# One core: w_out's sums beside w_in2's, joint low parts on GpSimd, w_out's loads a quarter step later

## The chip, the cores and the metric

The program runs on one core of a Trainium2 chip. Its time is the device time of one execution in microseconds (us). A core has TensorE (PE), which multiplies, VectorE (DVE), ScalarE (ACT) and GpSimd (POOL), which work on tiles, and queues that start DMA transfers: nearly all of them are started by SyncE (SP), a few by ACT. The program gives each engine and each queue a list of its own, and the trace shows its instructions in that order.

## The reference

```python
scores = (q @ k.T) / sqrt(64); ret = scores * gamma ** (i - j) for i >= j, else 0   # 8 x 8 heads, 576 positions
x = (ret @ v) as 4608 x 512
h = x @ w_in (512 x 2048);  g = h * sigmoid(1.702 * h);  x2 = g @ w_out (2048 x 512)
h = x2 @ w_in2;             g = h - tanh(h);             out = g @ w_out2
```

All data is float32. A product is taken as three passes on TensorE: each operand is split into a high part (fp32r, by a copy on ACT) and a low part (the operand less its high part, a subtraction), and high by high, high by low and low by high are summed.

## The kernel before

**Blocks and steps.** The 4608 tokens are 9 blocks of 512, and the 2048 columns of w_in are 16 chunks of 128. The first MLP's input products (`mm_in`, line 616, 12 matmuls each) are 144 steps, numbered by n; the main loop runs n = 32 to 143, and a step can be counted in the trace by its group of 12 L616 matmuls. Beside them the loop carries the rest of the attention (`attn_visit`, steps with even n up to 124), the decoding of the packed weights (`dec_piece`, a few pieces per step), the activation `act_a` (tanh on ACT, line 630, and a product on VectorE, line 632) and, for n = 34 to 81, the output products of the first three blocks (`out_units`, line 812, four units of three matmuls per step).

**Weights that are made on the way.** Some blocks are multiplied by a scheme with seven products in place of eight (Strassen's form), which needs sums and differences of parts of the weights. Two generators make them and are advanced once per step by `some(prep, 1)`: `w2_prep` forms those of w_in2 (its subtractions on GpSimd, line 960; copies and low parts at lines 938 and 939) and stores them as `wq`; `t_prep` forms those of w_out (half-tile subtractions on VectorE, line 995; copies and low parts at lines 990 and 991) and stores them as `wt`. They are chained: `t_prep` starts when `w2_prep` has ended. By the program's order `w2_prep` works in steps 49 to 104 and `t_prep` in steps 105 to 131. Each has 8 rounds. Both use the four halves of `room` in turn, and so does `sums`.

**The summed blocks.** In steps 96 to 111 and 128 to 143 (`SUMMED`), `sums` forms five operands of 128x512 from the activations of two blocks for every two steps (lines 1233 to 1236) and `stores` sends them to DRAM (line 1206, `gs`); the activations of other late blocks go there too (line 659, `gd`). A tile `t` that act_a writes is free for the next but two only when its store has landed.

**After the main loop** the second MLP's input products (lines 1046 and 1059) and the output products (`out_units`) take turns, a few units at a time. A step of `out_units` is four units of three matmuls. The steps that follow the first three blocks are: two more single blocks (line 812), then the joint stage of 56 steps for four blocks at once (`mm_joint`, line 753; seven stages of eight steps), then single blocks again (line 816). In the joint stage every step needs two activations: each is loaded (`g_load`, line 723, into one of five buffers), copied on ACT (line 728) and subtracted on VectorE (line 729) by `act_b`. At the end of a stage `evac_joint` empties the four accumulators; in the last five stages VectorE does it (line 786), adding a `kept` tile that `kept_load` (line 770) fetched when five steps of the stage were done. Before an accumulator is emptied, the next stage's first matmuls into it can't start, where that stage begins afresh.

**Order of the loads.** `w_ahead(k)` starts the load of the weights of a later step (line 272; line 286 in the joint stage: two steps ahead, into the slot that the step before the present one has read). It stands at the start of step k, ahead of `g_ahead`, which starts the loads of activations and their splits. All of these are SP's, so a load that waits for its slot holds up whatever stands behind it.

```python
def w_ahead(k):                   # out_units calls it first in a step
    if joint(k + 2): wj_load(k + 2 - N1)
    while n_w[0] <= min(k + 3, n_steps - 1): ... wo_load(n_w[0])
def g_ahead(x):
    while ... n_g[0] <= ...: g_load(n_g[0])      # SP: load
    while ... n_b[0] < n_items: act_b(n_b[0])    # ACT copy, then the low part
```

## Time and profile before

| | |
|---|---|
| three runs | 1701.92, 1705.47, 1706.06 us; median 1705.47 |
| profiled execution | 1705.2 us, its span 1703.4 us |
| TensorE busy | 1651.0 us (97%), mean granted clock 0.99 |
| VectorE, ScalarE, GpSimd busy | 1228.3 us (72%), 886.6 us (52%), 110.6 us (6%) |
| DMA | 510.60 MB, mean 300 GB/s |

The span runs from the first to the last instruction; 1.8 us of the time lie outside it. A busy time is the sum of an engine's instructions; the time of the whole follows the engine that waits least, here TensorE, and so the waits of TensorE and the stretches in which it does fewer matmuls than elsewhere are what there is to read. Lines are those of the kernel before.

### The profile page before, as it was taken

What the parts mean: (1) busy time and instruction counts of PE and PEld (TensorE: products, weight loads), DVE (VectorE), ACT (ScalarE), POOL (GpSimd) and SP (SyncE); (2) the same over time, 40 slices, a digit from 0 to 9 for tenths busy, and PEclk for the clock granted to TensorE, in tenths of its full rate; (3) what the DMA queues carried; (4) which work ended last, traced back from release to release, by engine and by line L of the source; (5) the groups of instructions that cost most, each with busy time, mean ns of one, the idle gap of its engine ahead of it and who ended that gap; (6) DMA issues with size and microseconds to landing.
All of it is one profiled execution on the core that took longest, in us unless ns stands there. A gap on an engine that the chain in (4) does not pass through costs nothing.

```text
span 1703.4 us, 25300 instructions
## 1 busy us (share of the span) xinstructions
PE 1651.0 (97%) x8874; PEld 1342.8 (79%) x8874; DVE 1228.3 (72%) x1958; ACT 886.6 (52%) x1633; POOL 110.6 (6%) x99
## 2 busy tenths in 40 slices
PE   7999999999999998899999998999999999999999
PEld 4787888887888787688778777778888888888887
DVE  6787887778877866567678887777876777766632
ACT  5443433434433232456677666656665676656632
POOL 2101001212123100000000000000000000000000
PEclk9999999999999999999999999999999999999999
DMA  9666679888899989998899988989899988989962
GB/s 274 180 211 228 226 262 326 285 293 324 310 351 337 363 316 362 325 340 281 296 347 313 342 292 312 342 286 359 307 328 346 316 303 312 320 304 311 360 212 87
DMA packets 195503, 510.60 MB, mean 300 GB/s; under 512 B 21808, under 2 KB 31152, under 8 KB 186416
## 3 DMA queue, kind: packets, MB, share of 16 engines
q1 hardware_dynamic: 182704, 486.88, 82.2%
q10 hardware_dynamic: 12672, 22.11, 3.5%
q8 instruction: 70, 1.15, 0.3%
q14 instruction: 57, 0.47, 0.1%
HBM read 361.05 MB, written 147.85 MB: 299 GB/s over the span
## 4 chain that ended last, share of the span: by engine, by line
PE 75%; DMA 12%; DVE 8%; ACT 2%; issue 2%; SPq 1%; ACTq 0%; DVEq 0%
PE acc L816 23%; PE h L616 14%; PE acc L812 12%; PE x L1059 8%; PE acc L753 5%; PE y L1059 4%; PE h L1046 2%; PE w L1059 2%; DMA gs<-spare 2%; DMA gs<-t 1%; DMA gl<-gs 1%; DMA wos<-wd 1%; PE pat L538 1%; DMA gl<-gd 1%; DVE t L632 1%
## 5 line engine op out<-in xcount | busy, mean ns | idle before, releaser
L616 PE MATMUL h<-xh,wi 128*128 128x512 f32 x1152 | 372.3, 394 | 6.6 <-DVE t L632 5.8
L816 PE MATMUL acc<-wos,g 128*128 128x512 f32 x1344 | 329.6, 390 | 4.0 <-DVE kept L786 3.9
L816 PEld LDWEIGHTS acc<-wos,g 128*128 128x128 f32 x1344 | 252.4, 188 | 57.4 <-DVE kept L786 4.4
L728 ACT ACTIVATE g<-gl 128x512 fp32r<-128x512 f32 x222 | 139.3, 628 | 268.1 <-PE acc L816 173.2
L616 PEld LDWEIGHTS h<-xh,wi 128*128 128x128 f32 x1152 | 217.3, 189 | 56.3 <-DVE t L632 7.1
L729 DVE TENSOR_TENSOR g<-gl,g 128x512 fp32r<-128x512 f32 x222 | 152.1, 686 | 147.0 <-ACT g L728 146.4
L616 PE MATMUL h<-xl,wi 128*128 128x512 f32 x576 | 225.4, 391 | 0.4 <-DVE xl L445 0.4
L1059 PE MATMUL x<-xo,wq 128*128 128x512 f32 x768 | 195.1, 389 | 1.3 <-DVE h L1339 1.3
L812 PE MATMUL acc<-g,wos 128*128 128x512 f32 x768 | 189.0, 396 | 6.2 <-DMA wos<-wd 5.9
L812 PEld LDWEIGHTS acc<-g,wos 128*128 128x128 f32 x768 | 144.4, 190 | 39.2 <-issue 7.5
L1059 PEld LDWEIGHTS x<-xo,wq 128*128 128x128 f32 x768 | 144.0, 188 | 32.0 <-DVE h L1339 2.1
L131 ACT ACTIVATE e<-e,ebias 128x512 int32<-128x512 int32 x64 | 46.4, 724 | 208.1 <-DVE e L129 202.8
L632 DVE SCALAR_TENSOR_TENSOR t<-t,h 128x512 f32<-128x512 f32 x144 | 97.6, 682 | 54.4 <-ACT t L630 54.2
L653 DVE SCALAR_TENSOR_TENSOR pl<-pl,sq 128x512 f32<-128x512 f32 x144 | 99.5, 691 | 39.6 <-ACT pl L650 37.4
L630 ACT ACTIVATE t<-h 128x512 f32<-128x512 f32 x144 | 83.4, 587 | 85.1 <-PE h L616 59.9
L616 PEld LDWEIGHTS h<-xl,wi 128*128 128x128 f32 x576 | 108.7, 189 | 22.9 <-DVE xl L445 1.1
L655 DVE COPY_PREDICATED t<-marks,pl 128x512 f32<-128x512 int32 x144 | 109.4, 760 | 14.8
L753 PE MATMUL acc<-g,wos 128*128 128x512 f32 x408 | 104.9, 396 | 12.5 <-issue 3.7
L650 ACT ACTIVATE pl<-sq,abias 128x512 f32<-128x512 f32 x144 | 104.3, 724 | 4.7
L651 ACT ACTIVATE marks<-sq,sbias 128x512 f32<-128x512 f32 x144 | 102.0, 708 | 0.0
L753 PEld LDWEIGHTS acc<-g,wos 128*128 128x128 f32 x408 | 77.2, 191 | 31.2 <-issue 13.0
L1059 PE MATMUL y<-xo,wq 128*128 128x512 f32 x384 | 99.3, 395 | 0.0
(129 smaller groups left out, 2301.1 us busy)
## 6 DMA issues: line engine op xcount, KB each, us to landing
wos<-wd SPq DMA_DIRECT2D x176, 512.0 KB, 5.6
gd<-t SPq DMA_DIRECT2D x208, 256.0 KB, 5.2
gl<-gd SPq DMA_DIRECT2D x202, 256.0 KB, 5.3
wq<-wq SPq DMA_DIRECT2D x32, 1024.0 KB, 7.4
at<-in_attn_dram SPq DMA_DIRECT2D x29, 1024.0 KB, 6.6
stg<-in_w_dram SPq DMA_DIRECT2D x48, 512.0 KB, 6.7
wq<-wq SPq DMA_DIRECT2D x32, 768.0 KB, 8.9
wd<-ws SPq DMA_DIRECT2D x32, 512.0 KB, 5.4
```

Of the source, the lines that this page charges most:

```text
L616: nc.tensor.matmul(h, lhsT=win[f][:, a, k], rhs=xs[b][:, k], start=(n == 0), stop=(n == 3 * KD - 1))
L632: nc.vector.scalar_tensor_tensor(out=t, in0=t, scalar=1.0, in1=h, op0=ALU.add, op1=ALU.mult)
L650: nc.scalar.activation(out=pl, in_=sq, func=ACTF.Square, bias=abias)
L651: nc.scalar.activation(out=small, in_=sq, func=ACTF.Relu, bias=sbias, scale=-1.0)
L653: nc.vector.scalar_tensor_tensor(out=pl, in0=pl, scalar=CB, in1=sq, op0=ALU.add, op1=ALU.mult)
L655: nc.vector.copy_predicated(out=t, mask=small.bitcast(I32), data=pl)
L728: nc.scalar.activation(out=g[:, 0], in_=t, func=ACTF.Copy)
L729: nc.vector.tensor_tensor(out=g[:, 1], in0=t, in1=g[:, 0].bitcast(F32), op=ALU.subtract)
L753: nc.tensor.matmul(acc[y], lhsT=wo[:, a, m * P:(m + 1) * P], rhs=g[:, b], start=fresh and q == 0 and n == 0, stop=q == NF // 2 - 1 and n = ...
L812: nc.tensor.matmul(acc[m], lhsT=wh[:, m // 2, a, m % 2 * P:(m % 2 + 1) * P], rhs=g[:, b], start=first, stop=last)
L816: nc.tensor.matmul(acc[m], lhsT=g[:, a, c], rhs=wo[:, b], start=first, stop=last)
L1059: nc.tensor.matmul(ps, lhsT=wq[q][t][:, o // 2, o % 2 * 2 + k, a], rhs=xo[i][k][:, b], start=first and n == 0, stop=n == 5, skip_group_che ...
```

## The change

Four things are changed. `t_prep` is no longer chained behind `w2_prep`: both are advanced in every step, and `t_prep` starts a round when the decoding has come far enough, as `w2_prep` does. By the program's order it now works in steps 49 to 88, and `w2_prep`, with one more `yield` in a round, in steps 49 to 112. Buffers move with that: `w2_prep` loads into the fourth half of `room`, both share the other three, `t_prep` loads into the tiles `gl`, and `sums` writes into tiles `stg`. The low parts of the joint stage's activations are formed on GpSimd. In a step of `out_units`, `w_ahead` stands after the first unit (ahead of `mm_out(o, 1)` or `mm_joint(k, 1)`), behind `g_ahead`; `kept_load` stands ahead of the step's fourth unit.

```diff
@@ -726,7 +726,8 @@
         t = tt.pop(step_of(x)) if x < DIRECT * NF else gl.pop(x)
         gt[x] = g = g_place(x)
         nc.scalar.activation(out=g[:, 0], in_=t, func=ACTF.Copy)
-        nc.vector.tensor_tensor(out=g[:, 1], in0=t, in1=g[:, 0].bitcast(F32), op=ALU.subtract)
+        eng = nc.gpsimd if joint_item(x) else nc.vector
+        eng.tensor_tensor(out=g[:, 1], in0=t, in1=g[:, 0].bitcast(F32), op=ALU.subtract)
 
     STAGES = (
         ("a11", ("o", 0, 0), True, None, "m1"),
@@ -880,12 +881,14 @@
     def out_units():
 
         for k in range(n_steps):
-            w_ahead(k)
             if joint(k):
-                kept_load(k)
                 for y in range(4):
                     if y % 2 == 0:
                         g_ahead(N1 + 2 * (k - N1) + y // 2)
+                    if y == 1:
+                        w_ahead(k)
+                    if y == 3:
+                        kept_load(k)
                     mm_joint(k, y)
                     if (k - N1) % (NF // 2) == NF // 2 - 1:
                         evac_joint(k, y)
@@ -894,6 +897,8 @@
             g_ahead(k if k < N1 else k + NJ)
             o = plain(k)
             for m in range(4):
+                if m == 1:
+                    w_ahead(k)
                 mm_out(o, m)
                 if o % NF == NF - 1:
                     evac(o, m)
@@ -931,7 +936,7 @@
                 )
 
         def halves_of(n, src):
-            sv = room[seen["room"] % 4]
+            sv = room[seen["room"] % 3]
             seen["room"] += 1
             kv = sv.rearrange("p a (k c) -> p (a k) c", c=2 * P).rearrange("p k (a c) -> p k a c", a=2)
             src = src.rearrange("p (k c) -> p k c", k=KD)
@@ -940,7 +945,8 @@
             waiting.append((n, sv))
 
         def load(q):
-            raw[q] = [t_p.tile([P, DM], F32, tag="gl", name="wr", bufs=2) for _ in range(2)]
+            t = room[3].bitcast(F32)
+            raw[q] = [t[:, 0], t[:, 1]]
             for i in range(2):
                 nc.sync.dma_start(out=raw[q][i], in_=w2_d[q + i * NF // 2])
 
@@ -948,6 +954,7 @@
             while n_dec[0] < 3 * (2 * NF + 2 * q + 3):
                 yield
             load(q)
+            yield
             yield
             wq_d[q] = dram.tile([P, 8 * DM], F32, tag=f"wq{q}", name="wq")
             lo, hi = raw.pop(q)
@@ -983,7 +990,7 @@
                 )
 
         def halves_of(n, src):
-            sv = room[seen["room"] % 4]
+            sv = room[seen["room"] % 3]
             seen["room"] += 1
             kv = by_half(sv)
             src = columns(src)
@@ -993,18 +1000,17 @@
 
         h = slice(0, DM // 2), slice(DM // 2, DM)
         sub = lambda o, a, b: nc.vector.tensor_tensor(out=o, in0=a, in1=b, op=ALU.subtract)
-        def load(q):
-            t = raw[q] = st_p.tile([P, 2, DM], F32, tag="stg", name="wr", bufs=3)
+        while not room:
+            yield
+        for q in range(NF // 2):
+            while n_dec[0] < 3 * (NF + q + NF // 2 + 3):
+                yield
+            wt_d[q] = dram.tile([P, 4 * DM], F32, tag=f"wt{q}", name="wt")
+            lo, hi = ts = [t_p.tile([P, DM], F32, tag="gl", name="wr", bufs=2) for _ in range(2)]
             for i in range(2):
-                nc.sync.dma_start(out=t[:, i], in_=r_d[q + i * NF // 2])
-
-        for q in range(2):
-            load(q)
-            yield
-        for q in range(NF // 2):
-            wt_d[q] = dram.tile([P, 4 * DM], F32, tag=f"wt{q}", name="wt")
-            t = raw.pop(q)
-            lo, hi = t[:, 0], t[:, 1]
+                nc.sync.dma_start(out=ts[i], in_=r_d[q + i * NF // 2])
+            yield
+            yield
             sub(lo[:, h[0]], lo[:, h[1]], lo[:, h[0]])
             sub(lo[:, h[1]], hi[:, h[1]], lo[:, h[1]])
             yield
@@ -1014,8 +1020,6 @@
             yield
             store()
             halves_of(1, hi)
-            if q + 2 < NF // 2:
-                load(q + 2)
             yield
             store()
 
@@ -1227,8 +1231,7 @@
         j = SUMMED[b]
         a11, a12 = firsts.pop(u)
         a21, a22 = (tt.pop(j * NF + q + i * NF // 2) for i in range(2))
-        s = room[seen["room"] % 4].bitcast(F32)
-        seen["room"] += 1
+        s = st_p.tile([P, 2, BLK], F32, tag="stg", name="s12", bufs=3)
         s1, s2 = s[:, 0], s[:, 1]
         nc.vector.tensor_tensor(out=s1, in0=a21, in1=a22, op=ALU.add)
         nc.vector.tensor_tensor(out=s2, in0=s1, in1=a11, op=ALU.subtract)
@@ -1242,7 +1245,7 @@
 
     room = []
     seen["room"] = 0
-    prep = chain(w2_prep(), t_prep())
+    prep, prep_t = w2_prep(), t_prep()
     std = x2_std()
     xo_tag += [f"wi{f}" for f in range(NF)] + ["ws", "ws"]
     outs = out_units()
@@ -1288,6 +1291,7 @@
             spare = [x_p.tile([P, 2, 2, DM], F32R, tag="y", name="spare", bufs=2) for _ in range(2)]
             room += [spare[i][:, k] for k in range(2) for i in range(2)]
         some(prep, 1)
+        some(prep_t, 1)
         if n == NB * NF - 6:
             w_ahead(DIRECT * NF - 2)
             while n_g[0] < DIRECT * NF + 3:
```

`w2_prep`'s `halves_of`, too, takes `seen["room"] % 3`. TensorE's order is the same in both programs. Three places show what moves elsewhere.

VectorE, end of step 50, and step 51, of the main loop (`L632` begins what a step adds; `L939` and `L944` are w_in2's low parts, `L1002` and `L998` w_out's subtractions and low parts). Before:

```order
L729 TENSOR_TENSOR g<-t,g 128x512
L137 SCALAR_TENSOR_TENSOR z<-stg,z 128x512
L939 TENSOR_TENSOR spare<-wr,spare 128x4x128
L143 SCALAR_TENSOR_TENSOR e<-stg,e 128x512
L148 TENSOR_TENSOR z<-z,e 128x512
L632 SCALAR_TENSOR_TENSOR t<-t,h 128x512
L729 TENSOR_TENSOR g<-t,g 128x512
L129 TENSOR_SCALAR e<-stg 128x512
L132 TENSOR_SCALAR z<-stg 128x512
L137 SCALAR_TENSOR_TENSOR z<-stg,z 128x512
L939 TENSOR_TENSOR spare<-wr,spare 128x4x128
L556 TENSOR_TENSOR xl<-pat,xh 128x4x128
```

and now:

```order
L1002 TENSOR_TENSOR wr<-wr 128x256 x2
L143 SCALAR_TENSOR_TENSOR e<-stg,e 128x512
L148 TENSOR_TENSOR z<-z,e 128x512
L632 SCALAR_TENSOR_TENSOR t<-t,h 128x512
L730 TENSOR_TENSOR g<-t,g 128x512
L129 TENSOR_SCALAR e<-stg 128x512
L132 TENSOR_SCALAR z<-stg 128x512
L137 SCALAR_TENSOR_TENSOR z<-stg,z 128x512
L944 TENSOR_TENSOR spare<-spare 128x4x128
L1002 TENSOR_TENSOR wr<-wr 128x256 x2
L998 TENSOR_TENSOR spare<-wr,spare 128x2x256
L556 TENSOR_TENSOR xl<-pat,xh 128x4x128
```

Two pairs of half-tile subtractions and a low part of w_out now stand here, behind step 50's and step 51's activation.

VectorE at the first stage end with kept tiles (`L786` and `L787` empty the accumulators; `L729` is a low part of the joint stage; the rest is the activation of the second MLP). Before:

```order
L729 TENSOR_TENSOR wos<-gl,wos 128x512 x2
L1339 TENSOR_TENSOR h_9029<-y,u_8990 128x512
L729 TENSOR_TENSOR g<-gl,g 128x512
L1339 TENSOR_TENSOR h_9052<-x,m_8955 128x512
L729 TENSOR_TENSOR g<-wos,g 128x512
L729 TENSOR_TENSOR g<-gl,g 128x512
L786 SCALAR_TENSOR_TENSOR kept<-acc_8759,kept 128x512
L649 TENSOR_TENSOR t<-h_9029,t 128x512
L653 SCALAR_TENSOR_TENSOR pl<-pl,sq 128x512
L654 SCALAR_TENSOR_TENSOR pl<-pl,h_9029 128x512
L655 COPY_PREDICATED t<-marks,pl 128x512
L1339 TENSOR_TENSOR h_9097<-w,m_8914 128x512
```

and now:

```order
L1343 TENSOR_TENSOR h_9029<-y,u_8998 128x512
L1343 TENSOR_TENSOR h_9060<-x,m_8962 128x512
L787 SCALAR_TENSOR_TENSOR kept<-acc_8766,kept 128x512
L649 TENSOR_TENSOR t<-h_9029,t 128x512
L653 SCALAR_TENSOR_TENSOR pl<-pl,sq 128x512
L654 SCALAR_TENSOR_TENSOR pl<-pl,h_9029 128x512
L655 COPY_PREDICATED t<-marks,pl 128x512
L1343 TENSOR_TENSOR h_9104<-w,m_8922 128x512
```

The low parts (`L729`) are gone from VectorE's order; nothing has come in their place.

SP at the same stage end (`gl` and `wos<-gs` are loads of activations, `wos<-wt` those of weights, `gd` the stores of activations, `wq` the weights of w_in2). Before:

```order
L659 DMA gd<-t 128x512
L723 DMA gl<-gs 128x512
L659 DMA gd<-t 128x512
L286 DMA wos<-wt 128x512
L770 DMA kept<-kept 128x512 x2
L770 DMA t<-kept 128x512 x2
L723 DMA wos<-gs 128x512
L723 DMA gl<-gs 128x512
L1036 DMA wq<-wq 128x2048
L1036 DMA wq<-wq 128x1536
L286 DMA wos<-wt 128x512
L723 DMA gl<-gs 128x512 x2
```

and now:

```order
L659 DMA gd<-t 128x512
L723 DMA wos<-gs 128x512
L286 DMA wos<-wt 128x512
L723 DMA gl<-gs 128x512
L1040 DMA wq<-wq 128x2048
L1040 DMA wq<-wq 128x1536
L771 DMA kept<-kept 128x512 x2
L771 DMA t<-kept 128x512 x2
L723 DMA gl<-gs 128x512
L286 DMA wos<-wt 128x512
L723 DMA gl<-gs 128x512 x2
```

The kept tiles' four loads have moved behind a load of weights, two of activations and the two big loads of `wq`.

## Rows read from the trace of the kernel before

**Rows 1.** Page: the span, and mean GB/s in forty equal slices.
```profile
span 1703.4 us, 25300 instructions
...
GB/s 274 180 211 228 226 262 326 285 293 324 310 351 337 363 316 362 325 340 281 296 347 313 342 292 312 342 286 359 307 328 346 316 303 312 320 304 311 360 212 87
```

**Rows 2.** Busy time by stretch, with matmul counts, clock and DMA; columns in line one.
```profile
core 0: us, PE busy (x) PEld busy (x) DVE busy (x) ACT busy (x) POOL busy (x), PEclk, DMA share, GB/s
272.00:500.00 228.00, 227.70 (x1461) 184.08 (x1460) 185.95 (x302) 95.63 (x182) 47.68 (x43) 1.00 0.87 312
500.00:590.00 90.00, 88.45 (x687) 71.97 (x686) 65.05 (x106) 27.23 (x61) 22.41 (x20) 1.00 0.99 353
660.00:720.00 60.00, 48.97 (x192) 39.15 (x191) 32.08 (x50) 18.30 (x32) 0.00 (x0) 0.89 0.95 341
720.00:820.00 100.00, 100.00 (x443) 82.81 (x442) 65.28 (x96) 55.19 (x95) 0.00 (x0) 1.00 0.87 315
820.00:1120.00 300.00, 279.47 (x1197) 226.10 (x1196) 234.57 (x360) 200.21 (x349) 0.00 (x0) 0.98 0.91 318
1120.00:1600.00 480.00, 480.00 (x2120) 397.44 (x2119) 350.00 (x523) 311.72 (x539) 0.00 (x0) 1.00 0.92 322
```

**Rows 3.** Waits of TensorE, 500 to 1120 us: total, times, longest.
```profile
PE acc L812 <- DMA wos<-wd: 5.9, 1, 5.9
PE h L616 <- DVE t L632: 5.8, 2, 4.2
PE acc L753 <- DVE t L786: 4.8, 4, 2.9
PE acc L816 <- DVE kept L786: 3.9, 1, 3.9
PE acc L753 <- issue: 3.7, 1, 3.7
```

**Rows 4.** Timeline, 660 to 700 us: start, duration, instruction, idle time before it.
```profile
671.32 1.08 ACT L630 ACTIVATE t<-h 128x512 f32<-128x512 f32 x2 [7.06 <-DMA gs<-t]
...
689.02 1.26 SPq L272 DMA_DIRECT2D wos<-wd  x2
...
698.57 5.46 PE L812 MATMUL acc<-g,wos 128*128 128x512 f32 x12 [5.92 <-DMA wos<-wd]
```

**Rows 5.** Timeline at 387 us: a split on VectorE and the matmuls after it.
```profile
386.51 0.68 DVE L729 TENSOR_TENSOR g<-t,g 128x512 fp32r<-128x512 f32 x1
...
387.42 1.75 PE L812 MATMUL acc<-g,wos 128*128 128x512 f32 x7
```

**Rows 6.** VectorE by line and form, 500 to 660 us: count, busy, mean ns.
```profile
L995 DVE TENSOR_TENSOR wr<-wr 128x256 f32<-128x256 f32 x32 | 13.5, 421 | 0.6
L991 DVE TENSOR_TENSOR spare<-wr,spare 128x512 fp32r<-128x512 f32 x16 | 11.0, 686 | 5.3 <-ACT spare L990 5.3
```

**Rows 7.** The same, 820 to 1120 us.
```profile
L729 DVE TENSOR_TENSOR g<-gl,g 128x512 fp32r<-128x512 f32 x52 | 35.7, 686 | 12.4 <-ACT g L728 12.2
...
L655 DVE COPY_PREDICATED t<-marks,pl 128x512 f32<-128x512 int32 x43 | 32.6, 759 | 4.4
```

**Rows 8.** GpSimd by line and form, whole span.
```profile
L332 POOL TENSOR_TENSOR at<-at,qt_sb 128x512 f32<-128x512 f32 x33 | 46.3, 1404 | 317.6 <-DMA at<-in_attn_dram 302.7 <-PE h L616 8.6 <-PE pe L428 6.3
```

**Rows 9.** Timeline: the same VectorE instruction beside GpSimd and without it.
```profile
559.20 1.30 POOL L332 TENSOR_TENSOR at<-at,qt_sb 128x512 f32<-128x512 f32 x1 [11.65 <-DMA at<-in_attn_dram]
...
559.21 1.83 DVE L1234 TENSOR_TENSOR spare<-spare,a 128x512 f32<-128x512 f32 x1
...
643.92 0.69 DVE L1234 TENSOR_TENSOR spare<-spare,a 128x512 f32<-128x512 f32 x1
```

**Rows 10.** Timeline at the first stage end with kept tiles.
```profile
935.54 0.98 SPq L770 DMA_DIRECT2D kept<-kept  x2
...
938.71 1.71 SPq L1036 DMA_DIRECT2D wq<-wq  x2
...
945.82 0.69 DVE L786 SCALAR_TENSOR_TENSOR kept<-acc,kept 128x512 f32<-128x512 f32 x1
```

More of the change, by code (lines that the diff above doesn't have):

```diff
@@ L1 @@
 from contextlib import ExitStack
-from itertools import chain, islice
+from itertools import islice
 import concourse.bass as bass
@@ L995, in t_prep @@
         sub = lambda o, a, b: nc.vector.tensor_tensor(out=o, in0=a, in1=b, op=ALU.subtract)
-        def load(q):
-            t = raw[q] = st_p.tile([P, 2, DM], F32, tag="stg", name="wr", bufs=3)
-            for i in range(2):
-                nc.sync.dma_start(out=t[:, i], in_=r_d[q + i * NF // 2])
-        for q in range(2):
-            load(q)
+        while not room:
             yield
         for q in range(NF // 2):
+            while n_dec[0] < 3 * (NF + q + NF // 2 + 3):
+                yield
             wt_d[q] = dram.tile([P, 4 * DM], F32, tag=f"wt{q}", name="wt")
-            t = raw.pop(q)
-            lo, hi = t[:, 0], t[:, 1]
+            lo, hi = ts = [t_p.tile([P, DM], F32, tag="gl", name="wr", bufs=2) for _ in range(2)]
+            for i in range(2):
+                nc.sync.dma_start(out=ts[i], in_=r_d[q + i * NF // 2])
+            yield
+            yield
             sub(lo[:, h[0]], lo[:, h[1]], lo[:, h[0]])
@@ L1301 @@
             wq_load(0, True)
-    some(prep, 99)
+    assert next(prep, None) is None and next(prep_t, None) is None
     stores(1)
```

## The prediction

> **What bounds the kernel now.** I read the table of stretches first. The yardstick is 720 to 820 us, where TensorE is busy all the time at full clock and does 443 matmuls of one size in 100 us, 4.43 per us [rows 2]. From 660 to 720 us the same kind of matmul is done 192 times where 266 fit: 74 too few, 16.7 us lost, 11.0 of them idle and the rest at a granted clock of 0.89. From 820 to 1120 us it is 1197 for 1329: 132 too few, 29.8 us lost, 20.5 of them idle. From 500 to 590 us TensorE idles 1.55 us; from 272 to 500 us and from 1120 to 1600 us it loses nothing that counts [rows 2]. So some 48 us of 1703.4 can be won or made worse; the rest is TensorE's own work, whose order does not change.
>
> The list of TensorE's waits says what ended them [rows 3]: in the first place two waits for VectorE's activation (5.8 us) and one for weights (5.9 us); in the joint stage the emptying of accumulators (4.8 and 3.9 us, and the 3.7 us put down to issue, which end as the first emptied accumulator comes free). The timeline gives what lies behind the first two: ACT stood 7.06 us before a tanh because the store of an old tile `t` had not landed, and the weights that TensorE waited 5.92 us for were asked for only at 689.02 us, 9.5 us before it could go on at 698.57 [rows 4].
>
> **w_out's sums, in their new place (272 to 500 us).** `t_prep` has 32 half-tile subtractions at 421 ns and 16 low parts at 686 ns, 13.5 + 11.0 = 24.5 us of VectorE [rows 6]. They go into steps 49 to 88. `w2_prep` has eight steps a round in place of seven, so 0.7 of a round, some 2 us, leaves that stretch. VectorE goes from 186 to about 208 us of 228, 82 to 91% [rows 2]. The cover is the time between a step's split and the matmul that reads it, and it is thin in places: at 387 us the split ended at 387.19 and TensorE began at 387.42 [rows 5]. What comes at the end of an odd step delays the next even one, where such places are; by the order that is 0.84 to 1.5 us more in about six of twenty. I take half a microsecond at three of them, **+1.5 us**. Bounds: 0, as the stretch loses nothing today at 82%, and 24.5 us if all of it came before TensorE. The ACT copies ahead of these low parts stand beside an ACT that is busy 96 of 228 us [rows 2]: nothing.
>
> DMA: 16 stores of 0.52 MB and 16 loads of 0.26 MB come in, 12.6 MB, and 1.8 MB of w_in2's go out: 10.8 MB in 228 us, 47 GB/s on 312 [rows 2], 359 in all. Slices of 42.6 us have reached 363 GB/s [rows 1], so it fits barely; no wait of TensorE there is for a transfer now, and I cost it at nothing. If that cover goes, each load of weights is late by its excess: that is the second rival below. The Trainium skill (SBUF — State Buffer, "A bandwidth-pool intuition that's wrong") gives some 358 GB/s for HBM to a core; by that figure the stretch would stand at the limit and the sum would be that rival's. The trace's slices go slightly over it, so I hold the rule right and the limit near.
>
> **Where they came from (500 to 720 us).** In steps 105 to 112 VectorE carried w_out's sums, low parts and `sums` together, and the 1.55 us at the end of that stretch are part of the wait for its activation [rows 2, 3]. With this work gone I take all of it, **−1.5 us** (0 to −1.55). At the second summed block (from step 128) only the last two rounds of `t_prep` are left to remove, some 1.0 to 1.6 MB of stores, at 353 GB/s [rows 2] 3 to 4.5 us of a DMA that carries 341 GB/s there through waits. The tanh that waited for its buffer [rows 4] can start that much earlier. The wait of 5.92 us stays: the weights' slot is freed by the store of the last sum, and neither that nor what it shares the DMA with has moved. **−4 us**, bounds 0 and −9 (the whole first wait with the slow clock behind it). What is late next is that load. `sums` now has three buffers for four; a buffer's last store is issued two steps (24 matmuls, 5.4 us) after the sum and comes round after six steps (16 us), so a landing may take ten: nothing.
>
> **The joint stage.** 112 low parts of 686 ns [rows 7], 76.8 us, leave VectorE, which is busy 234.6 of 300 us [rows 2]. They cost GpSimd, by the nearest row, 1404 ns each [rows 8], 157 us of 274: it keeps up at two per step. For the items themselves nothing is won: what they no longer wait in VectorE's queue GpSimd takes longer. What is won is VectorE's order: the low parts in front of `evac_joint` go. At the first end there are five in front of the first accumulator; many of these lie in time that VectorE waits anyway, so I take two per end on the path, 1.4 us, at five ends: −7. With shorter waits the clock falls less often: −2.
>
> Against it stands the port. The same subtraction of two SBUF tiles took 1.83 us beside a GpSimd instruction and 0.69 without one [rows 9]: it ended 0.55 us after GpSimd's, so it had waited for that. In the joint stage the 43 of line 655 [rows 7], as many of line 653 and some 18 others have two SBUF inputs. GpSimd runs over half of the time; half of 104 at half of 1.14 us is 30 us back on VectorE, spread like its work. At five ends two such stand between tanh and evacuation: I take **+2**. The Trainium skill says it as a rule (SBUF — State Buffer, "Who interferes with whom"): a VectorE instruction with two SBUF inputs and a GpSimd one that reads SBUF exclude each other for the whole instruction. By that rule, the trace agrees [rows 9], the gain is less than the moved 76.8 us, and where both instructions of an end meet it the sum is that of the third rival.
>
> `kept_load` three units later: at the first end the tiles were asked for at 935.54 us and used at 945.82 [rows 10]. Now they stand behind the two loads of `wq` of 938.71 (128x2048 and 128x1536 of four bytes, 1.84 MB, 5.2 us at 353 GB/s), as also at the fourth end by the order. They would land from about 946 to 949 us, so the first accumulator waits 0 to 3 us, and on VectorE all behind it. TensorE comes back to that accumulator some three units later; I take 1 us at two ends, **+2**. At the three others a delay of three units (15 matmuls, 3.4 us) fits in. The sum for the joint stage is −7 − 2 + 2 + 2 = **−5 us**. Bounds: the 18 us of evacuation waits and their clock won whole (−18), and the port and the kept tiles at their worst (+12, third rival).
>
> **Weights a quarter step later elsewhere.** From 1120 to 1600 us TensorE is busy 480.00 of 480 us [rows 2]; the loads run three steps ahead, of 20 matmuls or 4.5 us each, and one took 9.5 us at its worst above [rows 4]: 0. The loads of activations now stand before them, so SP waits for the same slot with less behind it. If the lead were too short, every step would show it.
>
> **Sum.** +1.5 − 1.5 − 4 − 5 = −9 on the profiled execution's 1705.2 us (span 1703.4 and 1.8 around it), which is 0.3 below the median of the runs: **1696 us**; by the bounds of the likely case 1689 to 1702.
>
> **Rivals.** *All evacuation waits go.* If it is VectorE's queue alone that makes them, the joint stage gives 18 us and not 5: 1683 us. For it: at the ends VectorE works without a gap in front of line 786. Against: the activation's own chain through ACT stands in between and stays.
>
> *The moved work comes back.* DMA at 359 GB/s and VectorE at 91% in 272 to 500 us: six late steps at 1.2 us give +7, the later stretches only −1.5 − 2, the joint stage −3: 1706 us, no change. For it: rows 5 and the sum of GB/s. Against: TensorE loses nothing there at 312.
>
> *Slower: port and kept tiles at the stage ends.* Each end gets both two-input instructions delayed by 1.14 us, 5 × 2.3 = 11.4, and at two ends 3 us of kept tiles, 6; 2 of clock, less 7 saved: +12 for −5, and 1713 us. It decides once more than about half of these instructions meet a running GpSimd one. For it: GpSimd gets its work from the same ACT copies at the same ends. Against: VectorE's lines run freely in the rest of the time.
>
> **How the numbers follow.** Forecast 0.43, first rival 0.17, second 0.20, third 0.20. Under 0.3% (5 us) a change of this kernel can't be told from none. Faster (under 1700.4): nine tenths of the forecast and the first rival, 0.56. Within 0.3%: a tenth of the forecast, most of the second rival, a quarter of the third, 0.26. Slower: the rest of both, 0.18. The range leaves out the lower tail of the first rival and the upper of the third: 1680 to 1711.
>
> **What would show it.** Right: 660 to 720 us with the 5.9 us wait alone and some 210 to 225 matmuls; 820 to 1120 us with 1215 to 1240; VectorE under 210 us there, GpSimd 140 to 180. Wrong: idle TensorE between 272 and 500 us (more than 3 us); waits for `kept` landings before line 786; a longer wait for `wos`; two-input instructions on VectorE that average over 1.2 us in the joint stage.

## The result, and the profile after

The changed kernel takes 1727.11 us (median of 4 runs, 1722.75 to 1728.51) against 1703.7 for the kernel before beside it: slower by 1.3% (ratio 1.0132, 95% interval 1.0108 to 1.0157). The forecast was 1696, its range ended at 1711. The profiled execution took 1728.51 us, its span 1726.7.

TensorE does the same 8874 matmuls in the same order, so the n-th of one trace is the n-th of the other, and the difference of their starts is a ledger. The changed kernel is 2.0 us behind at 272 us (of the kernel before), where nothing has been changed yet; the traces of the runs below lie 2.6 us before to 3.8 us behind the kernel before at that point. It loses **14.3 us from 272 to 545 us**, wins 3.3 from 545 to 705, loses nothing to 820, loses **10.3 from 820 to 1140** and 0.1 after that. The stretches, as [rows 2] have them:

```profile
core 0: us, PE busy (x) PEld busy (x) DVE busy (x) ACT busy (x) POOL busy (x), PEclk, DMA share, GB/s
272.00:500.00 228.00, 220.43 (x1380) 175.55 (x1380) 193.22 (x329) 95.99 (x184) 37.98 (x33) 1.00 0.93 332
500.00:590.00 90.00, 86.22 (x663) 70.05 (x663) 70.19 (x106) 31.22 (x65) 32.17 (x29) 1.00 1.00 363
660.00:720.00 60.00, 49.86 (x198) 39.81 (x197) 35.56 (x54) 16.72 (x29) 0.00 (x0) 0.91 1.03 372
820.00:1120.00 300.00, 282.41 (x1195) 229.38 (x1194) 215.07 (x239) 197.16 (x343) 168.89 (x112) 0.96 0.90 310
1120.00:1600.00 480.00, 472.28 (x2075) 390.31 (x2075) 346.23 (x517) 306.11 (x531) 0.70 (x1) 0.99 0.90 317
```

In the first stretch TensorE did 1461 matmuls before and does 1380 now: it is 7.6 us idle where it was idle for 0.3, and being late it has the last of that work still ahead of it. The 472.28 of the last row is the end of the joint stage, which now reaches past 1120 us. The waits, first from 272 to 500 us (total, times, longest):

```profile
PE acc L813 <- DVE g L730: 5.4, 8, 2.2
PE acc L813 <- ACT g L728: 2.2, 4, 0.9
```

and from 500 to 1160 us, where [rows 3] had 5.9, 5.8, 4.8, 3.9 and 3.7:

```profile
PE acc L754 <- DVE kept L787: 9.0, 3, 4.3
PE acc L817 <- DVE kept L787: 7.7, 1, 7.7
PE acc L813 <- DMA wos<-wd: 5.9, 1, 5.9
PE acc L754 <- DMA wos<-wt: 5.4, 3, 2.2
PE h L616 <- DVE t L632: 4.5, 2, 3.8
PE h L1050 <- DVE t L632: 3.5, 1, 3.5
```

All but 0.3 us of these twelve small waits for a step's high or low part are new in the early stretch. The longest wait at line 616 below, 3.8 us up to 518 us, belongs to them too. One of them, in the timeline (start, duration, instruction, idle time before):

```profile
292.89 0.63 ACT L997 ACTIVATE spare<-wr 128x512 fp32r<-128x512 f32 x1 [4.00 <-DMA wq<-spare]
...
293.56 1.00 DVE L998 TENSOR_TENSOR spare<-wr,spare 128x512 fp32r<-128x512 f32 x1 [3.94 <-ACT spare L997]
294.49 1.53 DVE L137 SCALAR_TENSOR_TENSOR z<-stg,z 128x512 f32<-128x512 uint32 x1
295.94 0.67 DVE L632 SCALAR_TENSOR_TENSOR t<-t,h 128x512 f32<-128x512 f32 x1
296.53 0.68 DVE L730 TENSOR_TENSOR g<-t,g 128x512 fp32r<-128x512 f32 x1
...
297.27 2.11 PE L813 MATMUL acc<-g,wos 128*128 128x512 f32 x8 [1.27 <-DVE g L730]
```

ACT stands 4 us at `t_prep`'s copy, because the half of `room` that it writes has not been stored; behind it VectorE stands, then works off what has queued, and the split that the matmul reads ends where the matmul begins. So the shared halves were my first suspect, VectorE's added work the rival, the transfers a third.

In the joint stage VectorE and GpSimd by line (count, busy, mean ns):

```profile
L655 DVE COPY_PREDICATED t<-marks,pl 128x512 f32<-128x512 int32 x42 | 44.1, 1051 | 4.3
L649 DVE TENSOR_TENSOR t<-h,t 128x512 f32<-128x512 f32 x32 | 39.6, 1236 | 33.4 <-ACT t L646 30.8 <-DMA gl<-gd 2.6
L653 DVE SCALAR_TENSOR_TENSOR pl<-pl,sq 128x512 f32<-128x512 f32 x42 | 36.1, 860 | 10.1 <-ACT pl L650 9.8
...
L730 POOL TENSOR_TENSOR wos<-gl,wos 128x512 fp32r<-128x512 f32 x44 | 67.8, 1550 | 45.0 <-ACT wos L728 41.3 <-DMA gl<-gs 3.5
```

Line 655 took 759 ns before [rows 7]; the other two, then:

```profile
L653 DVE SCALAR_TENSOR_TENSOR pl<-pl,sq 128x512 f32<-128x512 f32 x43 | 29.7, 690 | 14.2 <-ACT pl L650 14.0
...
L649 DVE TENSOR_TENSOR t<-h,t 128x512 f32<-128x512 f32 x32 | 22.0, 686 | 5.8 <-ACT t L646 5.8
```

TensorE's waits are only half of the joint stage's loss. The same matmuls, 820 to 1140 us of the kernel before and 833 to 1163.3 of the changed one (columns as in the stretches above):

```profile
820.00:1140.00 320.00, 299.47 (x1285) 242.67 (x1284) 249.77 (x383) 214.16 (x372) 0.00 (x0) 0.98 0.90 316
833.00:1163.30 330.30, 304.99 (x1284) 247.32 (x1283) 235.75 (x271) 214.24 (x372) 169.59 (x112) 0.95 0.89 307
```

TensorE is idle 25.3 us for 20.5, and busy 5.5 us longer with the same work, as its granted clock is lower: it stands at the lower of its two levels, half speed, for 30.7 us in place of 10.2. It falls five times, each time at the waits of a stage end. At the first, nine matmuls that took 2.20 us at 957.39 us take 3.98 at 966.61, right after the waits there.

At the first stage end with kept tiles, against [rows 10]:

```profile
948.90 0.90 SPq L1040 DMA_DIRECT2D wq<-wq  x2
949.85 1.15 SPq L771 DMA_DIRECT2D kept<-kept  x2
951.04 2.28 SPq L771 DMA_DIRECT2D t<-kept  x2
...
959.74 0.69 DVE L787 SCALAR_TENSOR_TENSOR kept<-acc,kept 128x512 f32<-128x512 f32 x1 [2.87 <-PE acc L754]
```

The tiles are asked for behind the `wq` pair and land some 10 us later, at 959.66; VectorE starts at 959.74 after 2.87 us idle. The row names the matmul, but the accumulator's last one ended near 956.2: the landing came last.

### The profile page after: what moved, and what is told of

Read it like the earlier page. It is cut to its first block, busy times and chain, and to the rows that moved or that the text cites. A ratio compares the mean times of both kernels' runs of the same rounds, so it can differ in the third digit from the quotient of the medians.

```text
span 1726.7 us, 25402 instructions
## 1 busy us (share of the span) xinstructions
PE 1661.1 (96%) x8874; PEld 1348.4 (78%) x8874; DVE 1220.7 (71%) x1846; ACT 886.9 (51%) x1633; POOL 284.5 (16%) x211
## 4 chain that ended last, share of the span: by engine, by line
PE 57%; DMA 7%; DVE 2%; SPq 1%; issue 1%; ACT 1%; POOL 1%; ACTq 0%; POOLq 0%; DVEq 0%
PE acc L817 23%; PE x L1063 8%; PE h L616 7%; PE acc L813 5%; PE acc L754 4%; PE y L1063 4%; PE h L1050 2%; PE w L1063 2%; DMA gd<-t 1%; DMA t<-kept 1%; DMA wos<-wd 1%; DMA wos<-wt 1%; DMA gs<-t 1%; DVE xo L924 1%; DMA kept<-kept 1%
## 5 line engine op out<-in xcount | busy, mean ns | idle before, releaser
L730 DVE TENSOR_TENSOR g<-gl,g 128x512 fp32r<-128x512 f32 x176 | 120.9, 689 | 140.4 <-ACT g L728 137.3
L813 PE MATMUL acc<-g,wos 128*128 128x512 f32 x768 | 191.5, 398 | 13.4 <-DMA wos<-wd 5.9
L813 PEld LDWEIGHTS acc<-g,wos 128*128 128x128 f32 x768 | 144.0, 190 | 49.8 <-ACT g L728 10.1
L632 DVE SCALAR_TENSOR_TENSOR t<-t,h 128x512 f32<-128x512 f32 x144 | 97.4, 682 | 68.2 <-ACT t L630 67.1
L649 DVE TENSOR_TENSOR t<-h,t 128x512 f32<-128x512 f32 x112 | 94.6, 844 | 67.1 <-ACT t L646 52.4
L655 DVE COPY_PREDICATED t<-marks,pl 128x512 f32<-128x512 int32 x144 | 121.7, 845 | 15.2 <-ACT g L728 0.5
L653 DVE SCALAR_TENSOR_TENSOR pl<-pl,sq 128x512 f32<-128x512 f32 x144 | 106.7, 741 | 34.9 <-ACT pl L650 32.0
L754 PE MATMUL acc<-g,wos 128*128 128x512 f32 x408 | 106.7, 402 | 11.2 <-DVE kept L787 6.4
L730 POOL TENSOR_TENSOR g<-gl,g 128x512 fp32r<-128x512 f32 x46 | 70.2, 1526 | 279.0 <-ACT g L728 278.9
L332 POOL TENSOR_TENSOR at<-at,qt_sb 128x512 f32<-128x512 f32 x33 | 47.2, 1432 | 351.3 <-DMA at<-in_attn_dram 274.3
```

What stands on the lines that cost most here:

```text
L632: nc.vector.scalar_tensor_tensor(out=t, in0=t, scalar=1.0, in1=h, op0=ALU.add, op1=ALU.mult)
L649: nc.vector.tensor_tensor(out=t, in0=h, in1=t, op=ALU.subtract)
L653: nc.vector.scalar_tensor_tensor(out=pl, in0=pl, scalar=CB, in1=sq, op0=ALU.add, op1=ALU.mult)
L655: nc.vector.copy_predicated(out=t, mask=small.bitcast(I32), data=pl)
L730: eng.tensor_tensor(out=g[:, 1], in0=t, in1=g[:, 0].bitcast(F32), op=ALU.subtract)
L754: nc.tensor.matmul(acc[y], lhsT=wo[:, a, m * P:(m + 1) * P], rhs=g[:, b], start=fresh and q == 0 and n == 0, stop=q == NF // 2 - 1 and n = ...
```

## The experiments

The ledger of every run against the kernel before, in us (plus is later), each from one profiled execution; the times are medians, beside medians of the kernel before of 1703.2 to 1706.6.

| kernel | time, us | ratio, 95% interval | 272–545 | 545–705 | 820–1140 |
|---|---|---|---|---|---|
| changed | 1727.1 | 1.0132 [1.0108, 1.0157] | +14.3 | −3.3 | +10.3 |
| undo_prep | 1712.2 | 1.0049 [1.0032, 1.0067] | 0.0 | −1.3 | +7.8 |
| undo_gp | 1732.1 | 1.0162 [1.0142, 1.0182] | +16.0 | −3.1 | +12.7 |
| undo_kept | 1721.0 | 1.0090 [1.0070, 1.0109] | +17.5 | −4.2 | +2.0 |
| undo_w | 1724.9 | 1.0117 [1.0097, 1.0137] | +16.1 | −5.3 | +9.0 |
| bufs_alone | 1731.2 | 1.0154 [1.0132, 1.0176] | +0.9 | +18.6 | +10.0 |
| t_dma | 1720.6 | 1.0091 [1.0069, 1.0113] | +9.3 | −3.3 | +10.3 |
| t_dma_subs | 1723.9 | 1.0107 [1.0087, 1.0127] | +11.7 | −3.5 | +10.3 |
| t_work | 1727.7 | 1.0136 [1.0113, 1.0158] | +17.5 | −5.2 | +9.5 |
| t_work_inplace | 1725.8 | 1.0124 [1.0082, 1.0166] | +13.4 | −2.9 | +13.8 |
| t_dve_only | 1717.0, one run | – | +9.2 | −2.8 | +7.4 |
| t_act_only | 1708.3, one run | – | +1.8 | −4.4 | +5.9 |
| gp_and_loads | 1706.0 | 1.0010 [0.9995, 1.0026] | 0.0 | +0.3 | +4.5 |
| gp_only | 1702.5 | 0.9992 [0.9980, 1.0004] | +0.1 | −3.6 | +0.8 |
| gp_half | 1702.2 | 0.9990 [0.9978, 1.0002] | 0.0 | −0.4 | −1.5 |
| gp_ends | 1700.05 | 0.9975 [0.9962, 0.9989] | +0.1 | −2.0 | −4.0 |
| gp_kept_early | 1713.1 | 1.0048 [1.0031, 1.0065] | 0.0 | −0.9 | +9.0 |
| kept_only | 1709.9 | 1.0035 [1.0022, 1.0048] | +0.1 | −1.8 | +5.9 |
| loads_only | 1708.6 | 1.0020 [1.0005, 1.0034] | +0.5 | −0.5 | +5.7 |

How far a column repeats: from 545 to 705 us gp_only, gp_half, gp_ends and kept_only run what the kernel before runs, and show −3.6 to −0.4. From 272 to 545 us undo_gp, undo_kept and undo_w run what the changed kernel runs, and the four show 14.3 to 17.5; TensorE's idle time there is 10.0 to 11.4 in all four (0.3 in the kernel before), and the time at the lower clock, 0 to 10.2 us, is what differs. From 820 to 1140 us undo_prep, bufs_alone and the six that begin with t_ run what the changed kernel runs, and show 5.9 to 13.8. So a difference of 3 us in the first column, and of less than some 8 in the last, can't be read from one trace alone. Two profiled executions lie well above their medians: loads_only's took 1715.3 us, 3.8 of it lost before 272 us, and t_work_inplace's 1732.5, where its other execution took 1719.0.

### One part of the change undone

**undo_prep**: `w2_prep`, `t_prep`, `room` and `sums` as before.
```
-        some(prep_t, 1)      # prep, prep_t = w2_prep(), t_prep()
+                             # prep = chain(w2_prep(), t_prep())
```


> The changed kernel with w_out's sums back behind w_in2's (from step 105 on, four halves of room shared in turn, the summed visits' s1 and s2 in room again); low parts on GpSimd, kept tiles and w_out's loads as changed. TensorE stood 14 us later at 505 us than in the kernel before and had won 3 us back by 705 us. Theory 1 (all of this is the moved sums): about 1727 - 11 = 1716 us, and TensorE 16 - 14 = 2 us behind the kernel before at 505 us. Rival (the loads a quarter step later take part of it, since the waits for wos from wt are 5.4 us there): those 5 us stay, 1721 us. Joint stage as in the changed kernel, +10 us.

1712.2 us, 15 less, and 0.0 lost from 272 to 545 us. The moved sums make the whole early loss; w_out's later loads have no part in it.

**undo_gp**: low parts on VectorE.
```
-        eng = nc.gpsimd if joint_item(x) else nc.vector
+        eng = nc.vector
```


> The changed kernel with the joint operands' low parts back on VectorE, all else as changed. The joint stage cost 10 us there. Theory G (VectorE's two-input instructions run longer beside GpSimd's, so tanh chain and evacuations are late): about 1727 - 10 = 1717 us, L649 back from 1220 to about 700 ns and L655 from 1037 to about 760 ns. Theory K (the kept tiles asked for later land 10 us later, so the evacuations at the stage ends wait): time stays at 1725 to 1730 us, and waits of VectorE for kept landings stay, 3 to 4 us each at two stage ends.

1732.1 us: slower, not faster. Lines 649 and 655 are back at 684 and 757 ns, as theory G had it, but the time is not:
```profile
L655 DVE COPY_PREDICATED t<-marks,pl 128x512 f32<-128x512 int32 x41 | 31.1, 757 | 4.2
...
L649 DVE TENSOR_TENSOR t<-h,t 128x512 f32<-128x512 f32 x32 | 21.9, 684 | 4.3 <-ACT t L646 4.3
```
The port slows VectorE as told, and yet the low parts' move does not cost the joint stage: beside the other parts it is worth 5.0 us by the medians. The ledger puts 2.4 of them in the joint stage, less than that column varies.

**undo_kept**: kept tiles at the start of the joint step.
```
+                kept_load(k)
                 for y in range(4):
-                    if y == 3:
-                        kept_load(k)
```


> The changed kernel with the kept tiles loaded at the start of the joint step again, ahead of the wq pair; all else as changed. Theory K (late landings of the kept tiles make the joint stage's 10 us): about 1727 - 10 = 1717 us, no idle VectorE ahead of the evacuations at stage ends, the waits of acc for kept (9.0 and 7.7 us over the run) nearly gone. Theory G (VectorE beside GpSimd): 1725 to 1728 us, the long waits at the stage ends stay with other names.

1721.0 us, 6.1 less, and the joint stage's loss falls from 10.3 to 2.0. Of TensorE's waits from 820 to 1160 us the three at line 754 for `kept` fall from 9.0 to 0.3 us, others grow, and the one at the last stage end stays:
```profile
PE acc L817 <- DVE kept L787: 7.6, 1, 7.6
PE acc L754 <- DMA wos<-wt: 5.8, 5, 1.9
...
PE acc L754 <- DVE kept L787: 0.3, 1, 0.3
```
Most of the gain in this trace is the clock. With the same matmuls as in the two rows above:
```profile
833.70:1155.80 322.10, 299.10 (x1285) 241.79 (x1284) 237.55 (x270) 213.88 (x372) 170.47 (x112) 0.98 0.90 314
```
TensorE is idle 2.3 us less than in the changed kernel and busy 5.9 us less; the lower level lasts 10.2 us, as in the kernel before.

**undo_w**: w_out's loads at the start of each step.
```
+            w_ahead(k)
-                    if y == 1:          # and m == 1
-                        w_ahead(k)
```


> The changed kernel with w_out's loads at the start of each step again, in all stages; the kept tiles stay late. TensorE waited 5.4 us for wos from wt in the changed kernel and 0.4 us for others of them; it no longer waited 4 us for wos from wd around 860 us as the kernel before did. If the quarter step costs: 1727 - 5 = 1722 us or below. If it is what took the wait around 860 us away: 1727 + 4 = 1731 us. If neither (the loads are hidden either way): 1725 to 1729 us.

1724.9 us; the 1.3 us that the joint stage has less are within what repeats, so in the whole time it can't be told from nothing. One place does answer: the wait at the last stage end falls from 7.7 to 4.9 us (see loads_only).

### What the early loss is made of

**bufs_alone**: the new buffers, `t_prep` after step 112.
```
-        some(prep_t, 1)
+        if n > 112:
+            some(prep_t, 2)
```


> The changed kernel with its new buffers (three halves of room in turn, the fourth holding w_in2's raw tiles, s1 and s2 in stg), but w_out's sums after w_in2's again, from step 113. Between 272 and 545 us TensorE fell 14 us behind the kernel before in the changed kernel, and 0 in the one that had neither. Theory B (the shared buffers make ScalarE and VectorE wait for stores): most of it, 8 to 14 us, is still lost there. Theory C (the sums themselves, their loads, stores and work): 0 to 3 us lost there, and 1712 to 1716 us in all.

0.9 us lost: the buffers alone cost nothing. (Its +18.6 later comes where the sums are now made, two pieces per step; that it is this is not shown.)

**t_dma**: loads and stores of `t_prep` only.
```
-            nc.scalar.activation(...); nc.vector.tensor_tensor(...)   # halves_of
-            sub(...)                                                  # four
+            for z in range(2): nc.sync.dma_start(out=wt_d[q][...], in_=src)
```


> The changed kernel, with w_out's sums reduced to their transfers: raw tiles are loaded and stored twice (as many bytes as the halves), without the subtractions, copies and splits, and without using room; so w_out's weights from wt are not the sums. Theory transfers (stores and loads at 359 GB/s are what is late): 8 to 14 us still lost between 272 and 545 us. Theory work (ScalarE and VectorE have no time left for them) or theory B (shared room): 0 to 4 us lost there, 1713 to 1717 us in all.

+9.3, 8.0 of it between 490 and 520 us, and 1.3 before; the changed kernel loses 10.2 of its 14.3 before 490. Around that place SP stands 12.7 us for stores out of the raw tiles (a wait that only this variant has), and a copy on ScalarE 10.5 us for the store of an old tile (440 to 560 us):
```profile
PE h L616 <- DVE t L632: 5.9, 2, 4.2
...
ACT spare L943 <- DMA gd<-t: 10.5, 1, 10.5
...
SPq L1004 <- DMA wt<-wr: 12.7, 4, 4.1
```
So transfers can cost much at that one place, though how much of it is this variant's own wait is open; what the changed kernel loses before 490 us they do not make.

**t_dma_subs**: the same with the four `sub`.


> As the run with w_out's sums reduced to their transfers, but with the four subtractions of each step on VectorE (31 of about 0.4 us); copies to high parts, splits and room are still left out. Theory work: a third of the loss, 3 to 6 us, comes with them. Theory B (what waits is the copy into a half whose store has not landed): 0 to 2 us more than without them.

+11.7, 2.4 more: less than the column varies, and no answer between the two theories.

**t_work**: all arithmetic, hardly a transfer.
```
+            if q == 0:  lo, hi = ... ; load
-                nc.sync.dma_start(out=wt_d[q]...)
+                stores_late.append(...)      # one a step from n = 113
```


> The changed kernel, w_out's sums with all their arithmetic from step 48 on, but with the raw tiles loaded once and the stores issued one a step from step 113; w_out's weights from wt are not the sums. Transfers alone cost 9.3 us between 272 and 545 us, transfers and subtractions 12, all of it 14. Theory transfers (they are what the 14 us come from, and the work adds to waits that are there): 1 to 4 us lost there. Theory work: 5 us or more lost there without them.

+17.5 with the DMA at 274 to 298 GB/s, as much as with the transfers: TensorE is idle 10.0 us, and 11.4 in the changed kernel. The work does it without the transfers, so theory transfers is out as the cause of the whole; 9.3 and 17.5 do not add to the 14.3.

**t_work_inplace**: the same without `room`.
```
-            nc.scalar.activation(out=kv[:, :, 0], in_=src, ...)
+            nc.scalar.activation(out=src, in_=src, ...)
```


> The run with w_out's sums without their transfers (17.5 us lost between 272 and 545 us), with the copy to the high part and the split written over the raw tile instead of into a half of room; as many instructions of as many columns on ScalarE and VectorE, and room is left to w_in2's sums alone. W_out's weights from wt are not the sums. Theory R (the shared room: an instruction waits for a half whose store has not landed, and its engine's queue with it): 0 to 5 us lost between 272 and 545 us. Theory work (ScalarE and VectorE lack the time): 12 to 17 us lost there.

+13.4, with TensorE idle 8.7 us for 10.0: the suspect of the timeline above, the shared halves, is not what makes most of the loss. The trace is the slower of two executions; the other was 13.5 us faster and left no trace. From 272 to 450 us ScalarE now stands for VectorE:
```profile
PE acc L813 <- DVE g L730: 2.5, 4, 1.0
PE acc L813 <- ACT g L728: 1.9, 2, 1.2
...
ACT wr L993 <- DVE wr L998: 15.6, 5, 6.9
```

**t_dve_only, t_act_only**: each engine's part of it.
```
-            nc.scalar.activation(out=src, in_=src, ...)      # t_dve_only
-            nc.vector.tensor_tensor(...); sub(...) x4        # t_act_only
```


> The run with w_out's sums' work in place and without transfers, 13.4 us lost between 272 and 545 us; here without its 16 copies on ScalarE, so VectorE's part alone (32 subtractions and 16 splits); w_out's weights from wt are not the sums. Theory V (VectorE lacks the time): 10 to 13 us still lost there. Theory Q (a copy waits on ScalarE for VectorE's subtraction, and the tanh, high parts and decode steps queued behind it are late; these waits were 22 us there): 0 to 5 us.

> The same, with the 16 copies on ScalarE alone, without VectorE's subtractions and splits. Theory V and theory Q both: 0 to 2 us lost between 272 and 545 us, since nothing stands on VectorE for a copy to wait for. Rival (ScalarE's own time): 4 us or more.

+9.2 for VectorE's part, +1.8 for ScalarE's, 13.4 for both; TensorE idles 6.4, 1.4 and 8.7 us. VectorE's part, without transfers and without `room`, is most of it. What is left for the queueing of one behind the other is less than the column varies. Either variant was measured once. TensorE's waits from 272 to 560 us with VectorE's part alone:
```profile
PE acc L813 <- DVE g L730: 4.6, 6, 1.7
PE acc L813 <- ACT g L728: 1.4, 2, 1.0
PE h L616 <- DVE t L632: 0.3, 1, 0.3
```

### One part of the change alone, and towards a better kernel

**gp_only, gp_and_loads**: the kernel before with the low parts on GpSimd; with w_out's later loads as well.


> The kernel before with one part of the change: the joint operands' low parts on GpSimd. With w_out's loads a quarter step later as well, TensorE gained 3.9 us by 880 us and lost it again, 6.2 us at the first stage end (920 to 950 us) and 3.6 at the last (1100 to 1120 us). Theory L (those losses come with the later loads of w_out's weights, and the waits for wos from wt with them): 1698 to 1701 us. Theory G (they come with GpSimd beside VectorE): 1705 to 1707 us, and the losses at the two ends stay.

> The kernel before with two parts of the change: low parts on GpSimd, w_out's loads a quarter step later. W_out's sums and the kept tiles' loads as before. The four runs that each undid one part give +15 us for the sums, +6 for the kept tiles, -5 for the low parts, +2 for w_out's loads. If they add: 1704 - 5 + 2 = 1701 us, within 2 us. If the low parts and the kept tiles hang together (a kept tile later in the queue only costs where the stage end is long): 1697 us or below.

1702.5 and 1706.0 us: the low parts alone can't be told from no change. In the joint stage TensorE idles 19.3 us for 20.5, and is busy 2.0 us longer at the lower clock. The 3.5 us between the two runs are the later loads' by the medians, but their intervals overlap.

**loads_only, kept_only**: the kernel before with `w_ahead` at the second unit; with `kept_load` at the fourth.


> The kernel before with one part of the change: w_out's loads at the second unit of each step, a quarter step later. Beside the low parts on GpSimd this part cost 3.5 us (1706.0 against 1702.5). Theory L (the weights land too late in the joint stage, whatever is beside it): 1706 to 1710 us, with waits for wos from wt of 3 to 5 us. Rival (it costs only beside GpSimd): 1703 to 1705 us.

> The kernel before with one part of the change: the kept tiles asked for at the fourth unit of the joint step. In the changed kernel this part cost 6 to 8 us, with the low parts on GpSimd. Theory K (a tile that lands late costs the stage end whatever stands beside it): 1704 + 6 = 1710 us, VectorE idle for kept tiles at two ends. Rival (it costs only where GpSimd and w_out's later loads crowd the same queue and port): 1704 to 1706 us.

Both cost by themselves: ratios 1.0020 and 1.0035, neither interval holds 1. The medians are 4.1 and 5.8 us above those of the kernel before, and the joint stage of the traces loses 5.7 and 5.9; undo_gp, which has both, loses 12.7 there. With kept_only 1.7 of the 5.9 are idle time of TensorE and 4.2 the lower clock, with loads_only 2.8 and 2.9. With loads_only the waits for `wos<-wt` are only 1.1 us; the last stage end is the longer one, 6.9 us for 3.9 [rows 3]. SP's order accounts for it. The kernel before, there:
```profile
1095.64 1.07 SPq L272 DMA_DIRECT2D wos<-wd  x2
...
1101.05 0.42 SPq L659 DMA_DIRECT2D gd<-t  x1
...
1105.39 0.63 ACT L646 ACTIVATE t<-h 128x512 f32<-128x512 f32 x1 [4.58 <-DMA gd<-t]
```
and with w_out's loads later:
```profile
1107.11 0.86 SPq L272 DMA_DIRECT2D wos<-wd  x2
1108.01 0.42 SPq L659 DMA_DIRECT2D gd<-t  x1
...
1114.76 0.63 ACT L646 ACTIVATE t<-h 128x512 f32<-128x512 f32 x1 [7.94 <-DMA gd<-t]
```
The second kernel was 6 us behind here already. But the pair of weights, 1 MB, was issued 5.4 us ahead of the store of `t` and now stands directly in front of it: the tanh that needs its buffer starts 6.75 us after the store's issue and no longer 4.34. It stands 7.94 us, and the evacuation comes behind its chain. In the changed kernel the same tanh stood 8.38 us and started 6.5 after the issue. This holds in every run: in the thirteen with the later loads the tanh stands 7.3 to 9.0 us there, in the seven without (undo_w among them) 4.5 to 6.0.

**gp_kept_early**: low parts on GpSimd, kept tiles one joint step earlier.
```
-        if name is None or q != NF // 2 - 3:
+        if name is None or q != NF // 2 - 4:
```


> The kernel before with the low parts on GpSimd and the kept tiles asked for one joint step earlier, where the change asked for them three quarters of a step later. Theory K (a stage end waits for its kept tiles, 3.9 us still in the kernel before): 2 to 4 us below the run with the low parts on GpSimd alone. Rival (they are in time in the kernel before, the waits there have the tanh chain behind them): no difference, within 2 us.

1713.1, 10.6 us over gp_only: both wrong. Two kept tiles sit in the ring of `t`; taken earlier, they are missing to the tanh. From 900 to 1130 us, where gp_only has 10.8 and 3.2:
```profile
ACT t L646 <- DMA gd<-t: 17.6, 5, 4.9
...
ACT t L646 <- DVE kept L787: 10.0, 2, 5.3
```

**gp_ends, gp_half**: only some of the low parts on GpSimd.
```
+        eng = nc.gpsimd if joint_item(x) and (x - N1) // 2 % (NF // 2) in (7, 0, 1) else nc.vector   # gp_ends
+        eng = nc.gpsimd if joint_item(x) and (x - N1) % 2 else nc.vector                             # gp_half
```


> The kernel before with the low parts on GpSimd for those operands alone that are formed around the end of a joint stage (steps 7, 0 and 1 of the eight); VectorE forms the others. Theory: what the part gains is the shorter VectorE queue ahead of the evacuations, and what it costs is the longer two-input instructions beside GpSimd; then this keeps the gain and loses less, 1698 to 1701 us. Rival (the gain is elsewhere, or gain and cost both are at the stage ends): 1702 to 1705 us, no different from the run with all of them on GpSimd.

> The kernel before with every second low part of the joint operands on GpSimd (those of the second of the two blocks). Theory (gain and cost go with the number moved): half of a small gain, 1702 to 1704 us. Rival (GpSimd's 1.5 us each is too slow for all, and half of them is enough to clear VectorE): 1699 to 1701 us.

gp_ends takes 1700.05 us against 1704.5, ratio 0.9975 [0.9962, 0.9989]: a quarter of a percent faster than the kernel before. Its interval overlaps gp_only's, so that it beats gp_only is not shown. VectorE runs nearer to its old times:
```profile
L655 DVE COPY_PREDICATED t<-marks,pl 128x512 f32<-128x512 int32 x44 | 34.6, 787 | 4.5
...
L649 DVE TENSOR_TENSOR t<-h,t 128x512 f32<-128x512 f32 x33 | 27.7, 839 | 21.1 <-ACT t L646 19.0 <-DMA gl<-gs 2.1
```

## Why the prediction was wrong, by its own steps

**w_out's sums, +1.5: failed; +14.3.** This is the step that decides. I took "half a microsecond at three of them"; it is twelve waits (5.4 and 2.2 us to 500 us) and a longer one behind them (3.8). I counted VectorE's room as an average, 82 to 91%, and it came out at 85%, so it was late without being full. And I read the thin places, as [rows 5], one by one. But the queue is in order: a group of added instructions, a copy on ScalarE that waits for one of them, the split behind both. VectorE's part alone costs 9.2 for 24.5 us of instructions, so more than a third of it came before TensorE (one execution). The bound (0 to 24.5) held it; the choice near zero had only "the stretch loses nothing today" behind it. The signal that I had named, over 3 us of idle TensorE there, came: 7.6.

**Transfers, 0: right up to 490 us, open behind it.** Alone they cost 1.3 by then, and 8.0 more at one place of a variant with a wait of its own; on top of the work they add nothing that shows (TensorE idle 11.4 with, 10.0 without). The stretch moved 332 GB/s, not 359, in part since the same work took 10 us longer.

**500 to 590, −1.5: the number came, the reason did not.** About 1.9 us go from 545 to 590 us in kept_only and gp_ends as well, which change nothing before the joint stage. The wait of 1.55 was one that comes and goes.

**660 to 720, −4: too much.** The 5.9 us wait stayed, as told; the tanh's is now 3.5 at line 1050; 198 matmuls, not 210 to 225 (though the kernel is 13 us behind there, so they are not the same matmuls). The 1.5 us won from 590 to 705 us are within what kernels show that change nothing there (−1.7 to +1.5 us).

**Joint stage, −5: failed; +10.3.** *The clock*: −2 came out as +5.5, the largest miss here. I let it fall less often for shorter waits, but the waits grew, and with them TensorE lost busy time at the lower clock: 304.99 us for 299.47. *Low parts*: −7, and +2 for the port. The port's instructions were told right and too small: lines 649, 653 and 655 got 17.6 + 7.1 + 12.3 = 37 us longer (counts by the rise of their means), and with lines 924, 654 and 1071 some 55, where I had 30; line 649, which I had not counted, passed the 1.2 us that I had named. With the clock, the sum is 0.8 alone (1.2 of idle time won, 2.0 lost by the clock) and −2.4 to −5.0 beside the other parts, not −7: that the chain behind a tanh became longer as the queue ahead of the evacuations became shorter is argued from the means, not shown. VectorE's busy time came out at 215 us, not under 210; GpSimd's 169 us were as forecast. The Trainium skill (SBUF — State Buffer, "Who interferes with whom") has it that a VectorE instruction with two SBUF inputs and a GpSimd one that reads SBUF exclude each other. The traces agree: line 649 takes 1236 ns in the changed kernel and 684 in undo_gp. *Kept tiles*: "the first accumulator waits 0 to 3 us" was nearly right (2.87 and 3.85 us), and "1 us at two ends" was as idle time of TensorE: 1.7 us alone (kept_only), 2.3 beside the rest (undo_kept). The price was 6 us by the medians, as the lower clock took 4.2 and 5.9 us more. *w_out's loads*: 0 here, and alone +5.7 by the ledger, 4.1 by the medians. I looked at the landing of the weights and not at what stands behind their issue on SP, the store that frees the tanh's buffer (6.75 us from issue to tanh for 4.34).

**Elsewhere, 0: right.** After 1140 us 0.1 is lost.

Of the rivals two came together: the second's place at twice its price, and the third's (+12 for +10.3), whose mechanism was half right: kept tiles, and SP's queue and the clock in place of the port. As I had put them, each was an alternative; here they were separate parts of one change, and both came.

## What to carry to other kernels

An engine that is 82% busy had no 18% to give where a matmul reads its output a quarter of a microsecond later; price added work by the share of it that stands before the consumer in the queue, and let an experiment with that engine's work alone tell. A load that is moved is also a place in an in-order queue: name the store behind it and who waits for its buffer. Read a wait of TensorE together with the granted clock behind it: here 4.8 us of added idle time in the joint stage came with 5.5 us of added busy time at the lower clock. And move work to a second engine where it shortens a queue that ends on the path: with the low parts around the stage ends alone the gain was clear of noise, with all of them it was not.

## What the runs showed that I had not expected

VectorE's slowdown beside GpSimd goes with its operands' place. With all the low parts on GpSimd, the same line with both inputs in SBUF and with one of them, x, in PSUM:
```profile
L649 DVE TENSOR_TENSOR t<-h,t 128x512 f32<-128x512 f32 x32 | 37.4, 1168 | 47.1 <-ACT t L646 44.3 <-DMA wq<-wq 2.8
...
L649 DVE TENSOR_TENSOR t<-x,t 128x512 f32<-128x512 f32 x11 | 7.5, 684 | 4.1 <-ACT sq L648 4.1
```
The one takes 1168 ns and the other 684, as without GpSimd. And a load moved earlier cost no less than one moved later: kept tiles a step earlier 10.6 us over gp_only, three units later 5.8 over the kernel before.
